# A decode kernel bound by its loads: fixed transpose buffers, a finer last block, and 256 rows of w_down loaded onto partitions 0 to 63 alone

## The chip, the cores and the metric

The kernel runs on one core of a Trainium2 chip. The metric is device time in microseconds (us) of one execution; every number of a run is a median with the lowest and highest execution beside it. One core draws its loads through sixteen DMA engines (the page of a profile counts 16). The trace does not name them; the numbers 0 to 15 in this text are names. The tensor engine is PE, the vector engine DVE, the scalar engine ACT, GpSimd POOL and the sync engine SP; SP issues nearly all loads here.

## The reference

For four tokens, `g * a + (1 - g) * b`. Cut to what matters:

```python
# A: attention over a cache: B=4, H=32 heads, 8192 cached positions, Dh=128, D=1024
q = (x @ wq)                                   # wq 1024 x 4096
p = softmax(q . k_cache / sqrt(128))           # k_cache, v_cache: 4 x 32 x 8192 x 128 bf16, 268 MB each
a = (p . v_cache) @ wo                         # wo 4096 x 1024
# B: one token per row, so every token is selected: F = 3584
b = x + sigmoid(x @ w_r) * ((silu(x @ w_gate) * (x @ w_up)) @ w_down)      # w_down 3584 x 1024
g = sigmoid((x * gate_w).sum(-1))
```

The inputs are 576 MB, nearly all of it the two caches, and each byte is used once.

## The kernel before

The program streams everything through a ring of five 4 MB buffers ("slots"). K loads and V loads alternate; the weights of part B are put in among the first of them ("side"), and `wo` comes last. Cut to what the change touches:

```python
ring = ctx.enter_context(tc.tile_pool(name="ring", bufs=5))      # 128 partitions x 32 KB each
ttp = ctx.enter_context(tc.tile_pool(name="ttp", bufs=2))        # transpose outputs, from a pool

def k_piece(u):
    ...
    kn = slot()
    nc.sync.dma_start(out=kn[:], in_=kv_view(A_k_cache, u))      # 4 MB: 128 rows of 32 KB
    for c in range(JR // CJ):                                    # 4 per piece, 256 in all
        T = ttp.tile([P, CJ, 2, 32, 2], BF, name="T", tag="T")
        nc.vector.transpose(out=T[:]..., in_=kn[:, c * CJ * Dh:(c + 1) * CJ * Dh]...)
        ...                                                      # matmuls on T

def wd_piece(g0, ng):                                            # w_down: ng groups of 512 rows
    w = slot()[:, :ng * FR * D]...
    nc.sync.dma_start(out=..., in_=wdv[:, g0:g0 + ng]...)        # 4 rows (8 KB) per partition and group
    ...                                                          # matmuls against hT

side = [..., lambda: (gu_piece(wuv, 1, TW), h_done()), lambda: wd_piece(0, 4), lambda: wd_piece(4, FG - 4)]
...
last = [wo_block(g) for g in range(2, NWB - 2)]                  # wo: 512 rows of 2 KB a block
last += [wo_block(g, r, r + FR // 2) for g in (NWB - 2, NWB - 1) for r in (0, FR // 2)]   # four halves
...
for use in last:
    use()                                                        # matmuls on wo, into acc
res = const.tile([Bn, D], BF)
nc.vector.tensor_copy(out=res[:, 0:NB], in_=acc[:, 0:NB])
nc.sync.dma_start(out=out2[:, 0:NB], in_=res[:, 0:NB])
... # the other half of res through ACT
```

## Time and profile before

| | before |
|---|---|
| time | 1349.41 us (1349.39 to 1349.46, 3 runs) |
| profiled execution | 1349.57 us, span 1347.8 us |
| DMA busy | 90% or more in 39 of 40 slices |
| PE, DVE busy | 79%, 47% |
| DMA rate | 428 GB/s, mean of the span |

These are lines of the profile's page of the kernel before. Part 2 cuts the span into 40 slices: one digit a slice is the busy share in tenths, and GB/s is what the sixteen engines moved. Part 3 has one line a DMA queue: packets, MB, share of the time of sixteen engines.

```profile
span 1347.8 us, 8253 instructions
...
PE   2667779876978868876998769888788859797878
...
DMA  9999999999999999999999999999999999999997
GB/s 403 433 433 422 433 430 430 432 433 430 430 433 430 430 431 434 429 431 432 433 428 432 433 430 430 433 431 429 432 434 429 428 433 434 429 428 434 432 423 323
DMA packets 22162, 576.22 MB, mean 428 GB/s; under 512 B 2399, under 2 KB 2407, under 8 KB 2925
...
q1 hardware_dynamic: 22104, 575.68, 99.5%
q8 instruction: 27, 0.44, 0.1%
q14 instruction: 11, 0.08, 0.0%
```

DMA is at 9 throughout and the rate is flat at about 431 GB/s: the loads bound the kernel, and compute hides under them. Only the last slice falls to 7 and 323 GB/s. Queue 1 carries the data; queues 8 and 14 carry the program itself, 27 and 11 packets of instructions. By its count queue 8 is taken to be the tensor engine's program (27 packets; the page has 4600 and 2412 instructions on PE and PEld); of queue 14, the five packets that fall together on one engine are taken to be DVE's.

The timeline of the kernel before, from 1342.3 us on, shows what comes after the last load (start, duration, engine, line, operation, in brackets the idle time before it and what ended it):

```profile
1342.57 1.02 PE L188 MATMUL acc<-piece,LT 128*4 128x512 bf16 x4 [0.17 <-DMA piece<-in_A_wo_dram]
...
1343.81 1.02 PE L188 MATMUL acc<-piece,LT 128*4 128x512 bf16 x4 [0.22 <-DMA piece<-in_A_wo_dram]
...
1344.66 0.68 DVE L461 CAST res<-acc 4x512 bf16<-4x512 f32 x1 [8.20 <-PE acc L188]
1344.87 0.57 ACT L463 CAST res<-acc 4x512 bf16<-4x512 f32 x1 [13.41 <-PE acc L188]
```

PE waits for the last half block of `wo`, which lands at 1343.77 us, then does four matmuls, and 4.1 us after the landing the span ends. So the span is "when the last load lands" plus 4.1 us.

**When does a load land?** Of each load onto all 128 partitions the trace has sixteen completion records, taken to be one from each engine. The distance from first to last record tells how far the engines have drifted apart. It was 1.2 us at the start of the stream, 2.1 at 258 us, 5.0 at 1133 us and 6.5 at the last transfer: the first engine is done at 1337.26 and the last at 1343.77. Six microseconds lie between the early engines and the late ones, and only the latest counts.

**Who is late?** Packet records of the trace carry a queue, a size, a start and a duration, but no engine. I reconstructed the engines by chaining packets, each starting where one of its engine ended. In the chains of before, three engines carry no instruction packets and end at 1336.8 to 1337.1 us; the eight that carry queue 8 in turn end at 1341.5 to 1341.8 (three packets) and 1342.9 to 1343.4 (four packets); one with five packets of queue 14 ends at 1342.8. So each queue-8 packet (16 KB; about 1.0 to 1.1 us itself) costs its engine about 1.5 us. From one 4 MB load to the next, the sixteen records keep their distances, except that one of them falls back by 1.52 to 1.56 us where a packet of queue 8 lies (20 of the 27 packets can be read so in the kernel before), and one by 0.95 to 0.98 us at each of the five packets that are taken to be DVE's. The record of a landing comes 0.4 to 0.5 us after its engine's last packet, so an end in the chains (1343.4) and a landing (1343.77) are not the same number.

That the packets of queue 8 go round eight engines can be seen without any chaining, from the durations of its 27 packets. Every eighth has nearly the same duration, but for the very first (ns, kernel before; the columns are turns 1 to 8):

```
turn       1     2     3     4     5     6     7     8
         964  1018  1026  1081  1069  1061  1100  1108
        1094  1018  1018  1073  1068  1061  1100  1099
        1095  1018  1018  1074  1069  1060  1099  1107
        1094  1018  1020
```

27 is three rounds and three more, so the engines of turns 1 to 3 have a fourth packet. Two neighbours in the ring are set apart by their 1013 to 1026 ns; they will be called the short pair.

### The profile page before, as it was taken

The page shows a single profiled execution, that of the slowest core. Times are in us where ns is not written, and L with a number is a line of the kernel's source. Part 1 is how long each engine was busy: PE and PEld are TensorE (multiplying, and loading weights), DVE is VectorE, ACT ScalarE, POOL GpSimd, SP SyncE. Part 2 cuts the span into 40 slices and gives each one's busy share as a digit, 9 for nine tenths or more (in the row PEclk, how much of TensorE's full clock was granted, in tenths as well). Part 3 has the DMA queues.
Part 4 walks back from the last instruction along what each step waited for, and adds up shares of the span by engine and source line. Part 5 has one row for each costly group of instructions (what it writes and reads, how often), then busy time and mean ns, then how long its engine had stood idle before and what let it go on. Part 6 is the DMA issues. An engine that isn't in the chain of part 4 may idle for free.

```text
span 1347.8 us, 8253 instructions
## 1 busy us (share of the span) xinstructions
PE 1059.3 (79%) x4600; PEld 233.2 (17%) x2412; DVE 631.4 (47%) x375; ACT 41.5 (3%) x46; POOL 47.9 (4%) x115
## 2 busy tenths in 40 slices
PE   2667779876978868876998769888788859797878
PEld 0111111211111111111212111211112112121111
DVE  3555755535544554454545454444544456346000
ACT  0000010001000010001000010000000010000000
POOL 2000000000000000000000000000000000000000
PEclk8878989898989989989898879899888979999899
DMA  9999999999999999999999999999999999999997
GB/s 403 433 433 422 433 430 430 432 433 430 430 433 430 430 431 434 429 431 432 433 428 432 433 430 430 433 431 429 432 434 429 428 433 434 429 428 434 432 423 323
DMA packets 22162, 576.22 MB, mean 428 GB/s; under 512 B 2399, under 2 KB 2407, under 8 KB 2925
## 3 DMA queue, kind: packets, MB, share of 16 engines
q1 hardware_dynamic: 22104, 575.68, 99.5%
q8 instruction: 27, 0.44, 0.1%
q14 instruction: 11, 0.08, 0.0%
q10 hardware_dynamic: 20, 0.02, 0.0%
HBM read 575.68 MB, written 0.01 MB: 427 GB/s over the span
## 4 chain that ended last, share of the span: by engine, by line
DMA 50%; PE 30%; DVE 11%; issue 6%; ACT 1%; POOL 1%; SPq 0%; DVEq 0%; ACTq 0%
DMA piece<-in_A_k_cache_dram 40%; PE o_ps L401 16%; PE S_ps L342 13%; DVE T L336 10%; DMA piece<-in_A_v_cache_dram 9%; PE small L419 1%; DMA piece<-in_A_wo_dram 1%; POOL PB L373 1%; DVE PT L367 1%; ACT PTs L365 1%; ACT OS L411 1%; DVE OS L412 1%; POOL tot L377 0%; PE acc L188 0%; PE o_ps L225 0%
## 5 line engine op out<-in xcount | busy, mean ns | idle before, releaser
L336 DVE STREAM_TRANSPOSE T<-piece 128x2048 uint32<-128x2048 uint32 x256 | 576.1, 2288 | 437.0 <-DMA piece<-in_A_k_cache_dram 321.1
L342 PE MATMUL S_ps<-T,Z 128*128 128x512 bf16 x2048 | 544.6, 416 | 246.6 <-DVE T L336 235.3
L401 PE MATMUL o_ps<-piece,PB 128*16 128x512 bf16 x2048 | 457.6, 382 | 14.8 <-DMA piece<-in_A_v_cache_dram 14.8
L342 PEld LDWEIGHTS <-Z 128*128 128x128 bf16 x1024 | 108.0, 105 | 667.2 <-issue 664.3
L401 PEld LDWEIGHTS <-PB 128*16 128x16 bf16 x1024 | 91.9, 90 | 373.1 <-issue 361.3
L412 DVE SCALAR_TENSOR_TENSOR OS<-o_ps,mE,OS 128x512 f32<-128x512 f32 x16 | 12.0, 751 | 174.6 <-ACT OS L411 174.6
L326 POOL TENSOR_TENSOR Z<-qa,mq 128x16 bf16<-128x16 bf16 x64 | 16.7, 262 | 1072.3 <-PE S_ps L342 1054.3
L411 ACT ACTIVATE OS<-o_ps,mE 128x512 f32<-128x512 f32 x16 | 11.0, 687 | 1040.5 <-PE o_ps L401 1040.5
L419 PEld LDWEIGHTS small<-selg,OS 128*128 128x128 f32 x128 | 24.9, 273 | 12.2 <-issue 11.1
L419 PE MATMUL small<-selg,OS 128*128 128x8 f32 x128 | 22.3, 302 | 0.0
L353 DVE TENSOR_REDUCE m<-S_ps 128x1 f32<-128x1024 f32 x8 | 9.8, 1225 | 15.9 <-PE S_ps L342 15.9
L188 PE MATMUL acc<-piece,LT 128*4 128x512 bf16 x64 | 14.9, 378 | 1.7 <-DMA piece<-in_A_wo_dram 1.6
L373 POOL COPY PB<-PT 64x1024 bf16<-64x1024 bf16 x8 | 15.1, 1884 | 29.1 <-DVE rex L375 29.1
L372 ACT COPY PB<-PT 64x1024 bf16<-64x1024 bf16 x8 | 15.3, 1908 | 10.6 <-DVE PT L367 10.6
L367 DVE STREAM_TRANSPOSE PT<-PTs 128x1024 bf16<-128x1024 bf16 x8 | 10.0, 1245 | 11.9 <-ACT PTs L365 11.9
L188 PE MATMUL acc<-piece,hT 128*4 128x512 bf16 x56 | 12.4, 379 | 0.0
L131 PE MATMUL small<-identb,x 6*128 6x6 bf16 x8 | 0.6, 194 | 14.2 <-DVE identb L128 14.2
L379 DVE RECIPROCAL rinv<-tot 128x16 f32<-128x16 f32 x8 | 2.0, 253 | 19.9 <-POOL tot L377 19.9
L365 ACT ACTIVATE PTs<-S_ps,negm 128x1024 bf16<-128x1024 f32 x8 | 8.9, 1113 | 70.0 <-DVE negm L362 70.0
L225 PE MATMUL S_ps<-piece,xw 128*4 128x512 bf16 x64 | 6.6, 591 | 3.0 <-DMA piece<-in_A_wq_dram 3.0
L422 DVE SCALAR_TENSOR_TENSOR OT<-small,sgb,rinv 128x8 bf16<-128x8 f32 x16 | 3.2, 202 | 11.7 <-PE small L419 11.7
L358 POOL PARTITION_ALL_REDUCE gmx<-mex x8 | 3.1, 390 | 81.9 <-issue 50.3
(72 smaller groups left out, 74.6 us busy)
## 6 DMA issues: line engine op xcount, KB each, us to landing
piece<-in_A_k_cache_dram SPq DMA_DIRECT2D x64, 4096.0 KB, 39.4
piece<-in_A_v_cache_dram SPq DMA_DIRECT2D x63, 4096.0 KB, 39.1
piece<-in_A_wq_dram SPq DMA_DIRECT2D x2, 4096.0 KB, 22.1
piece<-in_B_w_gate_dram SPq DMA_DIRECT2D x2, 3584.0 KB, 40.1
piece<-in_B_w_up_dram SPq DMA_DIRECT2D x2, 3584.0 KB, 34.6
piece<-in_A_wo_dram SPq DMA_DIRECT2D x6, 1024.0 KB
piece<-in_B_w_down_dram SPq DMA_DIRECT2D x1, 4096.0 KB, 35.6
piece<-in_A_v_cache_dram SPq DMA_DIRECT2D x4, 1024.0 KB, 32.6
```

The costliest lines, as they stand in the source:

```text
L188: nc.tensor.matmul(out_ap, lhsT=lhsT, rhs=rhs, start=start, stop=True, skip_group_check=True)
L326: nc.gpsimd.tensor_tensor(out=Z[:, :, 31:31 + P].rearrange("p e (s d c) -> p e s d c", s=HT, d=QH)[:, :, :, :, 0], in0=qa[:, :, h0:h0 + HT ...
L336: nc.vector.transpose(out=T[:].rearrange("p j h i e -> p (j h i e)").bitcast(U32), in_=kn[:, c * CJ * Dh:(c + 1) * CJ * Dh].bitcast(U32))
L342: nc.tensor.matmul(sps[:, z, :], lhsT=Z[:, he, s:s + P], rhs=T[:, 16 * z:16 * z + 16, half, :, e], start=(t == 0 and c == 0 and he == 0), ...
L365: nc.scalar.activation(out=PTs[:], in_=sps[:].rearrange("p z n -> p (z n)"), func=ACT.Exp, bias=negm[:, 0:1], scale=scale, accum_out=rs[:, ...
L367: nc.vector.transpose(out=PT[:].rearrange("p j i -> p (j i)"), in_=PTs[:])
L372: nc.scalar.copy(out=Bv[0:W, :, :, 0, :], in_=Pv[0:W])
L373: nc.gpsimd.tensor_copy(out=Bv[W:P, :, :, 1, :], in_=Pv[W:P])
L401: nc.tensor.matmul(o_ps[row:row + NM, e, :], lhsT=B_[:, JT * t + c, z, w].rearrange("p e s j -> p (e s j)"), rhs=vn[:, j0 * Dh:(j0 + 4) * ...
L411: nc.scalar.activation(out=o_sb[:], in_=o_ps[:, 0, :], func=ACT.Copy, scale=mE[:, 0:1])
L412: nc.vector.scalar_tensor_tensor(out=o_sb[:], in0=o_ps[:, 1, :], scalar=mE[:, 1:2], in1=o_sb[:], op0=ALU.mult, op1=ALU.add)
L419: nc.tensor.matmul(oT[:, :], lhsT=o_sb[:, q * Dh:(q + 1) * Dh], rhs=selg[:, q].rearrange("p t s -> p (t s)"), start=(q == 0), stop=(q == 3))
```

## The change

The intent has three parts. (1) The transposes write two fixed buffers rather than tiles of a pool, with the write-after-write order of a buffer's two users left to the waits that its readers need anyhow; this saves semaphore instructions on DVE (236 to 61 in the built program). (2) The last 512 rows of `w_down` are no longer 4 rows on each of 128 partitions: 256 rows stay on all partitions (2 rows each), and 256 rows go to partitions 0 to 63 (4 rows, 8 KB each), in two times four transfers of eight partitions. The author took these transfers to fall on the same eight engines each time, so that the other eight carry less. (3) The last half block of `wo` is loaded as two quarters, so that two matmuls rather than four follow the last landing.

```diff
-    ttp = ctx.enter_context(tc.tile_pool(name="ttp", bufs=2))
+    Tt = [const.tile([P, CJ * P], BF, name=f"T{i}") for i in range(2)]
+    turned = []
+    def turn(in_ap):
+        T = Tt[len(turned) % 2]
+        i = nc.vector.transpose(out=T[:].bitcast(U32), in_=in_ap.bitcast(U32)).ins
+        if len(turned) >= 2:
+            tc.declare_no_dep(i, turned[-2], reason="its readers are waited for")
+        turned.append(i)
+        return T[:].rearrange("p (j h i e) -> p j h i e", j=CJ, h=2, i=32)
 ... (other users of the pool's tiles take parts of Tt)
+    hTh = const.tile([P, 2, Bn], BF)
+    hTe = const.tile([P // 2, FR, Bn], BF)
 ... (h_done also transposes h for these two)
+    def wd_rest(g0):
+        w = slot()
 ...
+        nc.sync.dma_start(out=wa..., in_=wdv[:, g0:FG - 1]...)            # two whole groups
+        nc.sync.dma_start(out=wb..., in_=B_w_down[f0:f0 + 256]...)        # 2 rows a partition
+        def eighths(p0):
+            src = B_w_down[f0 + 256:f0 + 512].rearrange("(p r) n -> p (r n)", r=FR)
+            for i in range(4):
+                sl = slice(p0 + i, p0 + 32, 4)
+                nc.sync.dma_start(out=wc[sl].rearrange("p r n -> p (r n)"), in_=src[sl])
 ...
+        eighths(0)
+        side.insert(0, lambda: (eighths(32), use()))
 ...
-            lambda: (gu_piece(wuv, 1, TW), h_done()), lambda: wd_piece(0, 4), lambda: wd_piece(4, FG - 4)]
+            lambda: (gu_piece(wuv, 1, TW), h_done()), lambda: wd_piece(0, 4), lambda: wd_rest(4)]
 ...
-    last += [wo_block(g, r, r + FR // 2) for g in (NWB - 2, NWB - 1) for r in (0, FR // 2)]
+    last += [wo_block(NWB - 2, 0, 2), wo_block(NWB - 2, 2, 4)]
+    last += [wo_block(NWB - 1, 0, 2), wo_block(NWB - 1, 2, 3), wo_block(NWB - 1, 3, 4)]
```

More of the change, by code (lines that the diff above doesn't have):

```diff
@@ L194, in gates @@
         rg_ps = small([P, 2, Bn])
-        wrep = ttp.tile([P, 2, DT, P], BF, name="wrep", tag="T")
+        wrep = Tt[0][:, 0:2 * DT * P].rearrange("p (w t d) -> p w t d", w=2, t=DT)
         for i in range(2):
@@ L205, in add_x @@
     def add_x():
-        xf = ttp.tile([Bn, D], F32, name="xf", tag="T")
-        nc.vector.tensor_copy(out=xf[:], in_=x6[0:Bn])
+        xf = Tt[len(turned) % 2][0:Bn, 0:2 * D].bitcast(F32)
+        nc.vector.tensor_copy(out=xf, in_=x6[0:Bn])
         for n in range(NH):
@@ L233, in q_done @@
     def q_done():
-        qs = ttp.tile([P, 2, 4, P], BF, name="qs", tag="T")
-        nc.vector.tensor_copy(out=qs[:].rearrange("p z c d -> p z (c d)"), in_=q_ps[:])
+        qs = Tt[1][:, 0:1024].rearrange("p (z c d) -> p z c d", z=2, c=4)
+        nc.vector.tensor_copy(out=qs.rearrange("p z c d -> p z (c d)"), in_=q_ps[:])
         qt = small([P, 2, 4, 4, 32], BF)
@@ L253, in h_done @@
     def h_done():
-        h = ttp.tile([P, 2, 512], F32, name="h", tag="T")
-        nc.scalar.activation(out=h[:], in_=o_ps[:], func=ACT.Silu)
-        nc.vector.tensor_tensor(out=h[:], in0=h[:], in1=acc4[:], op=ALU.mult)
+        h = Tt[len(turned) % 2][:, 0:2048].bitcast(F32).rearrange("p (z n) -> p z n", z=2)
+        nc.scalar.activation(out=h, in_=o_ps[:], func=ACT.Silu)
+        nc.vector.tensor_tensor(out=h, in0=h, in1=acc4[:], op=ALU.mult)
         for z in range(2):
@@ L260, in h_done @@
                 nc.tensor.transpose(out=ht[:, r].rearrange("p k i -> p (k i)"), in_=h[:, z, r:512:FR], identity=ident[:])
-            kn = min(4, FG - 4 * z)
+            kn = min(4, FG - 1 - 4 * z)
             for r in range(FR):
@@ L264, in h_done, with use @@
                                         in1=c12[:, 1:2, :].to_broadcast([P, kn, Bn]), op=ALU.mult)
+        k6 = (FG - 1) % 4
+        for dst, rows, c0, nr in ((hTh, P, 0, 2), (hTe, P // 2, 256, FR)):
+            ht = small([rows, nr, 4, 32])
+            for r in range(nr):
+                nc.tensor.transpose(out=ht[:, r].rearrange("p k i -> p (k i)"), in_=h[:, 1, c0 + r:c0 + 256:nr],
+                                    identity=ident[:])
+            nc.vector.tensor_tensor(out=dst[:], in0=ht[:, :, k6, 0:Bn],
+                                    in1=c12[0:rows, 1:2, :].to_broadcast([rows, nr, Bn]), op=ALU.mult)
+    def wd_rest(g0):
+        w = slot()
+        f0 = P * FR * (FG - 1)
+        n2 = FG - 1 - g0
+        wa = w[:, 0:n2 * FR * D].rearrange("p (g r n) -> p g r n", g=n2, r=FR)
+        wb = w[:, n2 * FR * D:(n2 * FR + 2) * D].rearrange("p (r n) -> p r n", r=2)
+        wc = w[0:P // 2, (n2 * FR + 2) * D:(n2 * FR + 6) * D].rearrange("p (r n) -> p r n", r=FR)
+        nc.sync.dma_start(out=wa.rearrange("p g r n -> p g (r n)"),
+                          in_=wdv[:, g0:FG - 1].rearrange("f g r n -> f g (r n)"))
+        nc.sync.dma_start(out=wb.rearrange("p r n -> p (r n)"),
+                          in_=B_w_down[f0:f0 + 256].rearrange("(p r) n -> p (r n)", r=2))
+        def eighths(p0):
[3 more added lines that the diff above has]
+                nc.sync.dma_start(out=wc[sl].rearrange("p r n -> p (r n)"), in_=src[sl])
+        def use():
+            for lhs, rhs in [(hT[:, g0 + g, r, :], wa[:, g, r]) for g in range(n2) for r in range(FR)] \
+                    + [(hTh[:, r, :], wb[:, r]) for r in range(2)] + [(hTe[:, r, :], wc[:, r]) for r in range(FR)]:
+                for n in range(NH):
+                    mm_acc(acc[:, n * NB:(n + 1) * NB], lhs, rhs[:, n * NB:(n + 1) * NB])
+        eighths(0)
+        side.insert(0, lambda: (eighths(32), use()))
     def wd_piece(g0, ng):
@@ L334, in k_piece @@
         for c in range(JR // CJ):
-            T = ttp.tile([P, CJ, 2, 32, 2], BF, name="T", tag="T")
-            nc.vector.transpose(out=T[:].rearrange("p j h i e -> p (j h i e)").bitcast(U32),
-                                in_=kn[:, c * CJ * Dh:(c + 1) * CJ * Dh].bitcast(U32))
+            T = turn(kn[:, c * CJ * Dh:(c + 1) * CJ * Dh])
             s = 31 - (JT * t + c)
```

## The prediction

> **What bounds the kernel.** The DMA engines. The page's slices show them 90% or more busy in 39 of 40, 428 GB/s on average; the tensor engine 79%. A 32 KB packet takes 1.215 us (median of the packet records), and no engine's chain of packets shows a gap, so faster compute in the middle buys nothing. Each big DMA ends with 16 completion records, one per engine. First to last they lie 1.2 us apart at 12 us, 3.4 at 433, 5.0 at 1133 and 6.5 for the last transfer (seven engines by 1339.3 us, nine at 1342.0 to 1343.8). After the slowest come 1.0 us of four matmuls (timeline: 1343.81), a copy, the output, end at 1347.8.
>
> **Why engines lag.** The spread jumps at instruction fetches. Queue 8 fetches 27 times 16 KB[...]. Chaining packets end to start (my reconstruction; the trace names no engine), these rotate over eight engines, three or four each, about 1.6 us lost per fetch. A ninth engine carries five 8 KB fetches of queue 14[...], 1.2 us each: it ends at 1342.8, the slowest at 1343.4.[...]
>
> **What the change does.**
> 1. Fixed transpose buffers: the built program drops 175 vector-engine semaphore instructions (236 to 61); the engine's total goes from 616 to 443, so five fetches become three. That takes about 2.4 us off the ninth engine.
> 2. 256 rows of w_down (512 KB) move from all partitions to 0 to 63. [...] So engines 0 to 7 carry eight more 8 KB packets minus the halved rest: +1.2 us; engines 8 to 15 carry 1.2 us less (8 x 312 ns become 8 x 159 ns). If 8 to 15 are the fetching eight, their ends fall from 1341.5-1343.4 to 1340.3-1342.2; the ninth goes to about 1341.6, the early ones to at most 1340.3.
> 3. Finer end: the last half-block becomes two quarters: two matmuls after the last landing, not four, -0.4 us; eight more packets of 2 KB cost +0.1 us.
> 4. Costs: ten more transfers, some transposes, a slot held longer; the small transfers' semaphores delay one K load to when w_down's rest has landed, leaving about 10 us of queued work instead of 39. I expect no gap.
>
> **Sum:** -1.2 + 0.1 - 0.4, about -1.5 us: **1347.9 us**, range 1346.9 to 1349.3. Chances: faster by over 2% 0.005, within 2% 0.99, slower 0.005.
>
> **What would show it right.** Queue 8 stays near 27 fetches; queue 14 loses two; total bytes unchanged; the last transfers' completion spread falls from 6.5 to about 4 us or less; DMA stays 9s around 60 to 130 us; after the last landing two matmuls.
>
> **What would make it wrong.** The fetching engines are not 8 to 15: then slow engines gain load, +1 us. The delayed K load starves the queue near 100 us: some us slower. The ninth engine turns out slowest after +1.2 us: gain about 0.5.

The sum came to -1.2 + 0.1 - 0.4 = -1.5 us, from 1349.4 to 1347.9. But the -1.2 rests on an assumption, that transfers of eight rows all fall on one and the same eight engines and leave out the other eight; its "0 to 7" and "8 to 15" can be read as names for these two halves. The times in it are the trace's (medians on queue 1: 312 ns for a packet of 8 KB, 160 ns for one of 4 KB). What the trace of before shows of small transfers are counts: the load of x, of four rows, has four packets of 2 KB and four completion packets of 4 bytes. That 443 instructions of DVE make three fetches was an estimate too (616 had made five). For the +0.1 the profile after has 84 ns for a packet of 2 KB and 159 for one of 4 KB, so sixteen for eight come to 0.07 us an engine.

## The result, and the profile after

Ratios in this text are the mean time of one kernel's fast runs over that of the other's fast runs of the same rounds, so they are not quite the ratio of the medians quoted.

| | before | after |
|---|---|---|
| time, median (lowest to highest) | 1349.40 (1349.26 to 1349.46), 6 runs | 1349.35 (1348.65 to 1350.13), 6 runs |
| ratio | | 1.000, 95% interval 0.9987 to 1.0013 |

The time is the same. But the six executions after are not scattered around 1349.35: they are 1348.65, 1348.72, 1348.74 and 1349.95, 1350.03, 1350.13. There are **two levels**, 1.3 us apart, one below the kernel before and one above it, and the median falls between. The profiled execution was one of the lower level.

The page of the profile after, the same lines:

```profile
span 1347.0 us, 8114 instructions
...
PE   3667669876978868886998769788688869887788
...
DMA  9999999999999999999999999999999999999998
GB/s 401 433 430 427 430 428 435 432 429 431 433 432 429 433 432 429 432 433 430 430 433 433 428 432 433 433 429 431 430 433 433 431 427 433 436 431 425 434 425 334
DMA packets 22447, 576.21 MB, mean 428 GB/s; under 512 B 2494, under 2 KB 2502, under 8 KB 3276
...
q1 hardware_dynamic: 22392, 575.68, 99.6%
q8 instruction: 27, 0.44, 0.1%
q14 instruction: 8, 0.07, 0.0%
```

Queue 8 kept its 27 packets. Queue 14 lost two packets of 8 KB, as predicted: those taken to be DVE's are three rather than five. (The page counts 8 packets rather than 11; the third is one of 96 bytes that lies 0.13 us after the start of the span before and 0.07 us ahead of it after.) The completion packets of 4 bytes on queue 1 show the small transfers: 2388 before, which is sixteen for each of 149 loads onto all partitions and four for an output of four rows; 2484 after, 96 more, which is sixteen for each of two further such loads and eight for each of the eight transfers of eight rows. The bytes are the same, and DMA stays at 9 where the small transfers are (about 130 to 155 us, the fourth and fifth slice: 427 and 430 GB/s). The end, from the timeline after, from 1342.3 us on:

```profile
1342.07 1.89 PE L202 MATMUL acc<-piece,LT 128*4 128x512 bf16 x8
...
1343.78 0.68 DVE L511 CAST res<-acc 4x512 bf16<-4x512 f32 x1 [7.78 <-PE acc L202]
1343.99 0.57 ACT L513 CAST res<-acc 4x512 bf16<-4x512 f32 x1 [12.99 <-PE acc L202]
```

The last load lands at 1343.31 and the copies start 0.47 us later rather than 0.89; the span ends 3.7 us after the landing rather than 4.1. The finer end works as meant.

What did not work is the landing. The completion records of the last transfer, in order (us after 1330):

```
before         7.3  7.3  7.6  8.5 ... twelve more, up to 13.77    first to last 6.51
after, lower   6.3  6.6  9.0  9.7 ... twelve more, up to 13.31    first to last 7.02
```

The drift was to shrink from 6.5 to about 4 us. It grew. The two earliest records became earlier still, by 1.0 and 0.7 us, where nothing was to be gained, and the latest came down by 0.46 us only. In the reconstructed chains of this execution the two latest engines, at 1342.7 and 1342.8, are two that carry three packets of queue 8 *and* eight of the moved packets. The six other engines of queue 8 carry none of them and end at 1340.3 to 1340.6 (three packets) or 1342.0 to 1342.1 (four), about 1.2 us earlier than in the kernel before, as predicted. So a theory suggested itself before any experiment: two of the eight fetching engines are among those that carry the moved rows.

That would also explain two levels (theory L). If the ring of queue 8 starts at another engine in another execution, the loaded two get sometimes three packets and sometimes four, and only loaded engines make the difference visible. Rivals: the fixed buffers or the finer end bring the two levels; or the small transfers slow the queue.

### The profile page after: what moved, and what is told of

It reads as the page before. It is cut to its first block, busy times and chain, and to the rows that moved or that the text cites. A ratio compares the mean times of both kernels' runs of the same rounds, so it can differ in the third digit from the quotient of the medians.

```text
span 1347.0 us, 8114 instructions
## 1 busy us (share of the span) xinstructions
PE 1064.0 (79%) x4610; PEld 234.2 (17%) x2420; DVE 632.3 (47%) x377; ACT 41.5 (3%) x46; POOL 48.0 (4%) x115
## 2 busy tenths in 40 slices
DMA packets 22447, 576.21 MB, mean 428 GB/s; under 512 B 2494, under 2 KB 2502, under 8 KB 3276
## 4 chain that ended last, share of the span: by engine, by line
DMA 47%; PE 33%; DVE 16%; ACT 1%; issue 1%; POOL 1%; SPq 0%; DVEq 0%; ACTq 0%
DMA piece<-in_A_k_cache_dram 36%; PE o_ps L450 16%; PE S_ps L391 15%; DVE T L117 14%; DMA piece<-in_A_v_cache_dram 5%; DMA piece<-in_B_w_down_dram 3%; DMA piece<-in_A_wq_dram 2%; DMA piece<-in_A_wo_dram 1%; PE small L468 1%; POOL PB L422 1%; PE acc L202 1%; DVE OS L461 1%; ACT PTs L414 1%; ACT OS L460 1%; DVE PT L416 1%
```

## The experiments

Twelve runs were made, two of them repeats of a kernel (3 and 11; number 6 stands for two runs). All computed correct results, also the marker kernel. Each call ran its kernels on one chip, beside runs of the kernel before on that chip: medians 1349.40, 1349.42, 1349.41 and 1349.47 us, all within 1349.20 to 1349.69.

### 1. Number the engines with marker loads

The trace names no engine, but engines can be told apart by what is put on them. In the profiles so far a transfer of one, four or eight rows has one, four or eight completion packets, and a load onto all 128 partitions sixteen. The author's assumption was that loads of 1 to 15 rows, of 256 bytes each, take 1 to 15 engines, and each load those of the shorter ones and one more. Then every engine gets a number of marker packets of its own, from 15 down to 0, that can be read off its chain. This text calls the engine with 15-m markers engine m. These numbers are names, and say nothing of how the chip numbers its engines.

```diff
+    mk = [const.tile([n, P], BF, name=f"mark{n}") for n in range(1, 16)]
+    def mark(n):
+        nc.sync.dma_start(out=mk[n - 1][:], in_=A_wo[0:n, 0:P])
 ...
             k_piece(u)
+            if 12 <= u < 27:
+                mark(u - 11)
```

> The kernel before plus fifteen marker loads in the middle of the stream, the n-th of n rows of 256 bytes[...]. Theory L (the end is set by the engines that also fetch instructions, and they are not all in 8 to 15): of the eight engines that take turns at queue 8, two have numbers under 8 and six have numbers of 8 or more, probably 6 to 13; the vector engine's fetches (queue 14) sit on one engine under 8. Rival F (the fetching eight are 8 to 15, as predicted, and something else ate the gain): all eight have seven or fewer markers. Time within 2 us of before under both.

Measured: 1349.57 us (one run), within the 1349.28 to 1349.65 of the nine runs of the kernel before beside it, so the markers disturb nothing that can be measured. The chains, by number of markers:

```
engine   queue-8 packets at (us; duration about)    queue-14 packets    end of data (us)
 14      39, 433, 838, 1236                                             1343.4
  5      86, 497, 885, 1279      (1018 to 1026 ns)                      1343.4
  6      137, ...                (1018 ns)                              (chain mixed up later)
  9      193, 586, 983                                                  1341.7
 10      236, 644, 1037                                                 1341.9
 11      290, 687, 1088                                                 1341.9
 12      342, 736, ...                                                  (later part mixed up)
 13      391, 798, 1182                                                 1341.8
  3                                                 five                1342.8
  0, 1, 4                                           0, 1, 2             1338.5 to 1338.7
  7, 8, 15                                          none                1337.0, 1337.2, 1337.4
```

The chain of engine 2 was lost near 445 us, and after that two chains are mixed in part; the numbers come from the stretch before it. The fetching engines are **5, 6, 9, 10, 11, 12, 13 and 14**, in a ring in the order 9, 10, 11, 12, 13, 14, 5, 6. Two of them, the short pair, are below 8. The expectation had the count right (two below 8) and guessed other numbers. The trace agrees with the assumption as far as it can: a load of n rows has n marker packets, and the chains fit engines that are nested, each load on those of the load before it and one more; they fit no other arrangement that I tried. Which engines carry the packets of queues 8 and 14 is thus read from these chains alone.

### 2. Everything but the move

```diff
-            lambda: (gu_piece(wuv, 1, TW), h_done()), lambda: wd_piece(0, 4), lambda: wd_rest(4)]
+            lambda: (gu_piece(wuv, 1, TW), h_done()), lambda: wd_piece(0, 4), lambda: wd_piece(4, FG - 4)]
 (and h_done as before)
```

> The changed kernel without the move of w_down: fixed buffers and finer end alone. Theory L: the slowest engine is still one with four fetches of queue 8, so the last landing stays within 0.2 us of before; the finer end saves about 0.35 us after it: 1349.0 to 1349.2 us, on one level (all runs within 0.3 us), because three of the eight engines have four fetches whichever the turn starts with. Rival B (the two levels of the changed kernel, 1348.7 and 1350.0, come from the fixed buffers or the finer end): two levels about 1.3 us apart here too.

Measured: 1349.46 us (1349.30 to 1349.57, 5 runs), ratio 1.000, interval 0.9988 to 1.0013. **One level.** So the two levels come with the move. The time missed the expectation by 0.3 us: the span fell to 1347.3 to 1347.5, as it should with the finer end, but the time of an execution lies 2.05 us above its span instead of 1.7. What those 0.3 us outside the span are, the profile does not show (see 6). The last landing is 1343.82, as in the kernel before (1343.77), although the engine with DVE's instructions now ends at about 1340.4: four-packet engines of queue 8 stand in for it, at 1343.1 to 1343.4.

### 3. The changed kernel again, hoping for a profile of the upper level

> The changed kernel once more. Theory L: two levels, about 1348.7 and 1350.0 us. On the upper one an engine that got more of w_down also has four fetches of queue 8, on the lower one it has three; the profile's time must agree with its count. With three neighbours of eight having the fourth fetch and two of the eight on the loaded side, about half of the runs are on the upper level. Rival B or a stall at the small transfers: the level has nothing to do with the turn of the fetches.

Measured: 1349.94, 1348.66, 1348.61, 1349.99, 1348.56 us: the same two levels. The profile fell on 1349.94, the upper one. The durations of queue 8's 27 packets, in ns, in turns 1 to 8, of the two profiled executions of one and the same program:

```
turn              1     2     3     4     5     6     7     8
lower level     961  1107  1086  1018  1026  1082  1078  1060
               1108  1099  1082  1016  1026  1073  1069  1061
               1108  1099  1093  1018  1013  1201  1073  1060
               1099  1099  1087
upper level     947  1015  1018  1073  1076  1068  1099  1099
               1094  1018  1018  1074  1068  1058  1100  1100
               1094  1020  1026  1073  1069  1066  1096  1107
               1087  1016  1025
```

(One packet of the lower level, 1201 ns at turn 6, is out of line.) In the lower level the short pair, engines 5 and 6, is at turns 4 and 5 and has three packets each. In the upper level it is at turns 2 and 3 and has four. The ring is the same, its start is not. In the chains the pair ends at 1344.0 us in the upper level, where it ended at 1342.7 and 1342.8 in the lower. The timeline of the upper level's profile, from 1343 us on:

```profile
1342.77 2.39 PE L202 MATMUL acc<-piece,LT 128*4 128x512 bf16 x9
...
1344.98 0.68 DVE L511 CAST res<-acc 4x512 bf16<-4x512 f32 x1 [7.75 <-PE acc L202]
1345.19 0.57 ACT L513 CAST res<-acc 4x512 bf16<-4x512 f32 x1 [12.93 <-PE acc L202]
```

The first copy starts at 1344.98 rather than 1343.78: all of the 1.2 us between the levels is the last landing (1344.51 against 1343.31). (A packet of queue 8 costs its engine 1.5 us in a single step, so 0.3 us of the fourth packet do not show in this difference; why is not known.) Theory L is borne out in two profiles; its confirmation by taking the load off the pair is run 10.

### 4. Engines 0 to 5, with six rows a transfer

This kernel was drawn up together with run 1, before the numbers were known. If the ring was 6 to 13, as guessed then, the moved rows should go to engines 0 to 5 only: ten transfers of six partitions at a stride of ten, and one of four.

```diff
-            for i in range(4):
-                sl = slice(p0 + i, p0 + 32, 4)
+            for sl in parts:
                 nc.sync.dma_start(out=wc[sl].rearrange("p r n -> p (r n)"), in_=src[sl])
+        six = [slice(i, 60, 10) for i in range(10)] + [slice(60, 64)]
-        eighths(0)
-        side.insert(0, lambda: (eighths(32), use()))
+        sixths(six[:5])
+        side.insert(0, lambda: (sixths(six[5:]), use()))
```

> The changed kernel with the 256 rows sent by ten transfers of six partitions and one of four, instead of eight of eight: same bytes, same partitions[...]. Theory L with the fetching engines at 6 to 13: every fetching engine loses 1.2 us, none gains; engines 0 to 5 gain about 2.0 us and end at 1342.5 us at the latest (the one with the vector engine's fetches): one level at 1347.9 to 1348.4 us. If partitions rather than engine numbers count, or if the small transfers stall the stream: no better than the changed kernel, 1348.7 to 1350.0 on two levels.

Measured: 1353.43 us (1353.03 to 1354.51, 5 runs), ratio 1.0031: 4 us slower, a clear miss. This had nothing to do with instruction fetches. The fourth and fifth slice of its page (GB/s) show where:

```profile
GB/s 404 433 432 405 401 427 434 429 431 435 432 425 433 431 434 430 431 430 434 431 433 428 431 432 432 432 432 429 432 432 432 428 431 431 434 432 429 431 425 329
```

405 and 401 where the changed kernel has 427 and 430. Packets of the large loads were slow around the small transfers: 32 KB packets took up to 3.2 us instead of 1.215, and 84 of them over 1.24 us (11 in the changed kernel; table in 9). (Engine 5 is one of the ring by run 1, and one of the six that a load of six rows marks, so it would still carry moved rows; by the estimates, 2.0 us here and 1.2 in the changed kernel, that is 0.8 us more, the smaller part of this loss.)

### 5. The move alone

The kernel before plus the move; tiles from the pool and the coarse end as before.

> The kernel before with the move of w_down alone: pooled transpose buffers and the old end. Theory L: the engine of the vector engine's fetches (number 3 by the markers, below 8) still has five of them and now gets 1.2 us more, so it ends at about 1344.0 us in every run, as late as engines 5 and 6 do on the upper level. The two levels fall together: all runs at 1349.8 to 1350.4 us, 0.4 to 1.0 above before. If the fixed buffers do not matter to the end: two levels, about 1349.0 and 1350.3.

Measured: 1349.99 us (1349.56 to 1350.47, 5 runs), ratio 1.0004, interval 0.9992 to 1.0017. So the move alone does not help and, in its upper runs (1350.47 twice), costs 1 us. The expectation, all runs between 1349.8 and 1350.4, was met in part only: two runs lie below it (1349.56 and 1349.71) and two just above, so the levels came closer but did not fall together. The profile, with the short pair at turns 7 and 8, shows a last landing of 1344.13; in the chains the latest engine is the one with five packets of DVE's instructions, at 1343.7: it carries moved rows as well. That shows what the fixed buffers can do in this change, in the one execution profiled: they clear engine 3, but only with the move does engine 3 become the latest.

### 6. The finer end alone, and the fixed buffers alone

The edits are those parts of the diff above.

> The kernel before with the finer end alone. Span 0.3 us shorter in any case. If the 0.3 us that the run without the move lost outside the span come with the finer end: 1349.4, as before. If they do not: 1349.0 to 1349.15 us.

> The kernel before with the fixed buffers alone. Theory L: the vector engine's fetches fall from five to three, but the engine that carries them was not the slowest, so the last landing does not move: span as before within 0.15 us. If the 0.3 us outside the span come with the fixed buffers: 1349.7 us; if not: 1349.4.

Measured: finer end 1349.20 us (1349.10 to 1349.27, 5 runs), 0.2 us under the kernel before (1349.42, 9 runs, of which seven lie above all five of these); the span of the profiled run is 1347.5. Fixed buffers 1349.77 us (1349.75 to 1349.80, 5 runs), 0.35 us *above*. The span of the fixed buffers' run is 1347.7, no longer than that of before, and the time lies 2.05 us above it; so the 0.3 us outside the span come with the fixed buffers in runs 2 and 6. The changed kernel, which has them too, lies 1.71 us above its span in both profiled runs. I have no explanation for this, and it stays open. (The kernel of runs 10 and 11 lies 1.93 and 1.95 us above its span; its two profiles alone show an instruction packet of 8 KB after the end of the span, by 1.8 us. Runs 2 and 6 show none, so this does not explain theirs.) The last landing with the fixed buffers alone is 1343.67 us, with the engine of DVE's instructions two packets lighter in the chains (1340.4, from 1342.8): the gain that the prediction gave to the "ninth engine" is there and buys nothing by itself, because engines of queue 8 are later.

### 7. Engines 0 to 4, spread out in time

A second attempt at fewer engines, with one small transfer (five, three or two rows) after each of fifteen K loads rather than several in a row, into a buffer of its own. If the slowness of run 4 came from small transfers in a row or from the wait for a slot, it should go.

```diff
+    few = [slice(i, 50, 10) for i in range(10)] + [slice(50 + i, 62, 4) for i in range(4)] + [slice(62, 64)]
+    def wd_few(i):
 ...
+        nc.sync.dma_start(out=wc[few[i]].rearrange("p r n -> p (r n)"), in_=src[few[i]])
 ...
+            if 10 <= u < 10 + len(few):
+                wd_few(u - 10)
```

> The changed kernel with the 256 rows sent by ten transfers of five partitions, four of three and one of two, one at a time after each K load from the eleventh on, into a buffer of their own, so that none holds a slot or has to wait for the one ahead. By the markers engines 0 to 4 have no fetches of queue 8; they alone carry the rows now (3.1 us for engines 3 and 4, up to 4.6 us for 0 and 1, less 1.2). Theory L: all eight fetching engines lose 1.2 us whichever turn the fetches take, no engine ends after 1342.4 us: one level, 1347.9 to 1348.4 us, and no gap in the stream at 100 to 170 us. If the loss of the version with six-partition transfers came from small transfers as such and not from the queue running dry: again 1351 or more.

Measured: 1353.18 us (1352.67 to 1353.30, 5 runs), ratio 1.0027. Missed again by 5 us, and again by slow packets, now in small groups at each transfer: 599 packets of 32 KB over 1.24 us between 125 and 500 us, where the changed kernel has 11. So neither the row of small transfers nor the shared slot was it. What runs 4 and 7 have in common, and the changed kernel has not: the stride of ten, that is, the partitions on which the rows of one transfer lie. The next two runs change these partitions and keep the packets.

### 8. One edit: eight neighbouring partitions

The changed kernel's rows lie at a stride of four partitions, from partitions 0 to 3 and 32 to 35 on. The test gives each transfer eight neighbouring partitions, with the source rows that belong there, and changes nothing else: the number of packets (22447 on both pages, 2494 of them under 512 B), their sizes and their places in the queue are the same.

```diff
-                sl = slice(p0 + i, p0 + 32, 4)
+                sl = slice(p0 + 8 * i, p0 + 8 * i + 8)
```

> The changed kernel with one edit: each of its eight small transfers takes eight neighbouring partitions instead of every fourth. The same number of transfers, the same 8 KB packets, the same eight engines (each transfer has eight rows)[...]. Two kernels before this one (six and five partitions at a stride of ten) were 4 us slower because packets on all engines lengthened around the small transfers. [...]this one shows it too: 32 KB packets over 1.24 us near 130 to 160 us, 1 to 4 us slower than the changed kernel. If it does not (then the stride of the source, the number of rows or the moment do), it stays like the changed kernel: each execution at about 1348.7 or about 1350.0, span 1347.0 or 1348.2.

(The first outcome stands for "the partitions matter", the second for "they do not".)

Measured: 1354.69 us (1353.66 to 1355.94, 5 runs), ratio 1.0038, interval 1.0024 to 1.0051. One changed slice costs 5 us. So it matters which eight rows, and with them which partitions, go into one transfer; by what means is not shown. The GB/s line of its page:

```profile
GB/s 405 430 432 393 409 431 427 432 431 432 433 433 430 426 433 429 434 433 431 432 431 431 431 432 432 432 430 429 432 433 429 432 431 432 434 430 432 427 427 310
```

The fourth and fifth slice are at 393 and 409. 79 packets of 32 KB between 125 and 170 us are over 1.24 us, where the changed kernel has 2.

### 9. The changed kernel's stride, four partitions up

Run 8 changed both the spacing of a transfer's rows and the partitions on which they lie. To part these, the rows kept the stride of four and were moved up by four partitions (4 to 67, in a fixed buffer). The source rows and the packets are those of the changed kernel; run 10 has a fixed buffer as well and is not slow.

```diff
+    wc = const.tile([68, FR, D], BF)
+    nc.gpsimd.memset(wc[:], 0.0)
 ...
-                nc.sync.dma_start(out=wc[sl].rearrange("p r n -> p (r n)"), in_=src[sl])
+                nc.sync.dma_start(out=wc[p0 + i + 4:p0 + i + 33:4].rearrange("p r n -> p (r n)"), in_=src[sl])
 (hTe has 68 rows, of which the first four meet zeros; two constants live in Tt to make room)
```

> The changed kernel with its eight small transfers moved up by four partitions (partitions 4 to 67, in a fixed buffer)[...]. [...] this is as slow: about 1354, 60 to 80 packets of 32 KB over 1.24 us near 130 to 160 us. [...]it is like the changed kernel, 1348.7 or 1350.0, with 1 or 2 such packets.

(The first outcome, as slow as run 8, is for the place of the rows as the cause, the second for their spacing.)

Measured: 1354.45, 1354.63, 1351.10, 1351.19 us (ratio 1.0021, interval 1.0006 to 1.0036). Two levels once more, both above those of the changed kernel, by 2.4 and 4.5 us. Its line, the profile being of the upper level:

```profile
GB/s 403 432 432 408 414 430 432 430 432 430 432 432 433 432 430 431 429 433 433 429 433 431 432 432 430 432 431 431 432 431 432 429 431 432 433 433 430 429 426 296
```

So the stride of four is not enough: the same rows four partitions up slow packets too. How much, all in one table: over all packets of queue 1 that start between 120 and 500 us, the time above the median of their size in the whole run, summed and divided by sixteen engines. (A median that is 1 ns higher takes 0.3 us off a figure, so 0.6 and 0.9 are the same.)

| kernel | us per engine | packets of 32 KB over 1.24 us |
|---|---|---|
| before | 0.9 | 11 |
| changed kernel, lower and upper level | 0.9, 0.9 | 11, 11 |
| 128 rows in transfers of four, stride of four from 0 to 3 and 32 to 35 on (run 10) | 0.6 | 10 |
| six rows at a stride of ten (run 4) | 4.9 | 84 |
| five rows at a stride of ten (run 7) | 4.2 | 599 |
| eight neighbours (run 8) | 5.4 | 88 |
| stride of four, moved up by four (run 9) | 3.5 | 89 |

Run 8's figure is 1.9 us above run 9's, so close spacing may add something; a run that parts the two in the other way was not made. For run 9 the table accounts for 2.5 us of the 4.5 in the upper level: its first engine is done 2.8 us later than the changed kernel's, the latest 4.5 us later, and why the late ones lose more I have not found out.

### 10 and 11. The dose halved, onto engines 0 to 3

With the ring known, the move can be aimed. 128 rows move rather than 256, in eight transfers of four rows, so that engines 0 to 3, those that a load of four rows marks, carry them, none of which is in the ring; the rows lie on partitions 0 to 15 and 32 to 47, at the stride of four that cost nothing in the changed kernel. The other 384 rows of the group lie 3 on a partition.

```diff
-    hTh = const.tile([P, 2, Bn], BF)
-    hTe = const.tile([P // 2, FR, Bn], BF)
+    hTh = const.tile([P, 3, Bn], BF)
+    hTe = const.tile([48, FR, Bn], BF)
+    wc = const.tile([48, FR, D], BF)          # both zeroed; partitions 16 to 31 stay zero
 ...
-                          in_=B_w_down[f0:f0 + 256].rearrange("(p r) n -> p (r n)", r=2))
+                          in_=B_w_down[f0:f0 + 384].rearrange("(p r) n -> p (r n)", r=3))
         def eighths(p0):
-            src = B_w_down[f0 + 256:f0 + 512].rearrange("(p r) n -> p (r n)", r=FR)
-            for i in range(4):
-                sl = slice(p0 + i, p0 + 32, 4)
-                nc.sync.dma_start(out=wc[sl].rearrange("p r n -> p (r n)"), in_=src[sl])
+            r0 = f0 + 384 + 2 * p0
+            src = B_w_down[r0:r0 + 64].rearrange("(p r) n -> p (r n)", r=FR)
+            for i in range(4):
+                nc.sync.dma_start(out=wc[p0 + i:p0 + 16:4].rearrange("p r n -> p (r n)"), in_=src[i:16:4])
```

> The changed kernel with the dose halved and the target narrowed: 128 rows instead of 256 move, in eight transfers of four partitions (8 KB packets), so that only engines 0 to 3 carry them, which by the markers' run carry none of the tensor engine's fetches[...]. The buffer of the rows is a fixed one, so two constants moved into the transpose buffers. Engines 0 to 3 gain eight packets of 0.31 us and lose 8 times 0.08 us: +1.9 us; all others, the eight fetching ones among them, lose 0.6 us. Theory of the fetching engines 5, 6, 9 to 14: last landing 0.6 us earlier than in the kernel with fixed buffers and finer end alone (1343.8), about 1343.2 in every execution, engine 3 with the vector engine's three fetches at about 1342.3; times of one level, 1348.5 to 1348.9, and no upper level at 1350.0. Rival (the two levels come from the transposed buffers or the chip, not from where the bytes go): two levels about 1.3 us apart again. If 4-row transfers slow packets as five- and six-row ones did, 2 us slower.

Measured: 1348.67 us (1348.43 to 1349.19, 5 runs), ratio 0.9995, interval 0.9983 to 1.0008. The profiled run's span is 1346.6 us, its last landing 1342.89. There is no run near 1350.0. There were two sublevels, 1348.43 to 1348.67 and 1349.09 to 1349.19, so the kernel was run again:

> The kernel with 128 rows on engines 0 to 3 once more, for the interval and for its two sublevels of 1348.5 and 1349.1 (the profile of the first run fell on the lower). Expected: again five times between 1348.4 and 1349.2, none at 1350.0; last landing near 1342.9 in the lower, 0.5 us later in the upper sublevel if the profile falls there.

Measured: 1348.73 us (1348.52 to 1348.85, 5 runs), ratio 0.9995, interval 0.9982 to 1.0007, last landing 1343.17; one level this time. The upper sublevel of the first five has no profile and stays unexplained. The lines of the page of run 10 that answer to those above:

```profile
span 1346.6 us, 8130 instructions
...
GB/s 402 436 430 426 429 434 431 429 432 433 430 432 432 431 431 430 432 433 430 432 430 434 432 429 432 433 429 431 433 432 427 434 433 429 429 435 433 429 425 335
```

426 and 429 in the fourth and fifth slice: no slow stretch. Its page has 2462 packets under 512 B, 32 fewer than that of the changed kernel: four completion packets a small transfer instead of eight. All ten runs (1348.43 to 1349.19) are below all eighteen runs of the kernel before beside them (1349.29 to 1349.64). The gain of 0.7 us is 0.05%, and the interval of the ratio, which allows for more than the scatter, does not exclude 1. By its median it is the fastest kernel (the lower level of the changed kernel is as fast); no bigger gain should be claimed for it.

## Why the prediction was wrong

The prediction was 1347.9 us, range 1346.9 to 1349.3; the median was 1349.35. Two levels, 1348.7 and 1350.0, lie around it; the lower is inside the range. Point by point:

- **"The DMA engines bound it; the end is set by the engines that lag, and they lag by instruction fetches"**: right. The 1.2 us between two executions of one program go with one packet of 16 KB more on each of two engines (run 3).
- **"The ninth engine: five fetches become three, -2.4 us"**: right. Queue 14 lost two packets of 8 KB, and in the chains that engine ended at 1340.4 rather than 1342.8 with the fixed buffers alone (run 6). By the steps of the completion records, 0.95 to 0.98 us each, the two packets account for 1.9 of these 2.4 us; the rest is not explained. It is worth nothing there, and counts only where the move loads that engine (run 5).
- **"Engines 0 to 7 carry +1.2 us, engines 8 to 15 carry 1.2 us less"**: right. The ring's six engines above 7 end at 1340.3 to 1342.1 rather than 1341.5 to 1343.4, and engines 5 and 6 have eight of the moved packets each in the chains.
- **"If 8 to 15 are the fetching eight, their ends fall from 1341.5-1343.4 to 1340.3-1342.2"**: **this step failed.** It carried the whole term of -1.2 us. The fetching eight are 5, 6 and 9 to 14 (run 1). Engines 5 and 6 gained 1.2 us on top of their fetches and became the latest. The last landing moved not by -1.1 us (-1.2 for the engines, +0.1 for the smaller packets) but by -0.46 us when these two have three fetches, and by +0.74 when they have four. The prediction named this as what would make it wrong, "+1 us", but took the even split as its central case with nothing in the trace to say which engines were which. It could have been known to be open: the chains gave a count, not numbers. And it assumed one fixed ring; that its start differs between executions of one program was in no term.
- **"Finer end: -0.4, +0.1"**: right within 0.2. Landing to end of span 4.1 us became 3.7 us in both levels; alone, it gained 0.2 us, and its last landing (1343.78) shows nothing of the 0.1 us for smaller packets (run 6).
- **"I expect no gap"**: right. One K load waited 9.3 us in its queue for `w_down` and was issued at 116.88 us, yet the K loads around the small transfers land at their usual distance of 9.7 us (first records at 130.95, 140.72, 150.43 us).
- **"The spread falls from 6.5 to about 4"**: wrong, in consequence: 7.0 and 8.3.

The sum for the lower level closes: landing -0.46, after the landing -0.35 gives -0.8 us, and the profiled executions differ by 0.83 (1349.57 and 1348.74). For the upper level +0.74 and -0.35 give +0.4; measured 1349.94 against 1349.57.

Shown by runs: which engines fetch (chains, numbered by markers), that the levels need the move (runs 2, 6) and follow the place of engines 5 and 6 in the ring (run 3), that with the load on engines 0 to 3 the upper level goes and the landing falls by 0.6 to 0.9 us (runs 10, 11), that small transfers of the same packets slow the stream or do not by the partitions on which their rows lie (runs 8, 9: 88 and 89 packets of 32 KB over 1.24 us, against 11; in the upper level of run 9 the first engine is done 2.8 us later and the latest 4.5). Not shown: why some partitions cost this and others do not, and which engine writes which partitions. Open: the 0.3 us outside the span with fixed buffers; the sublevels of run 10; why the ring starts where it does (in fourteen profiles the short pair was at turns 2 and 3 six times, 7 and 8 six times, 4 and 5 twice, and nowhere else).

## What to carry to other kernels

When sixteen engines share a stream, the slowest decides (here the last of sixteen records lay 6.5 us after the first, and the span ended 4.1 us after it); before moving bytes off "the slow ones", number them, for example with loads of 1 to 15 rows, which cost nothing measurable here (1349.57 us). When a kernel's repeats fall into two groups, look at each group by itself: here the median said "no change" while the program gained 0.7 us in one and lost 0.6 in the other. And when a transfer has few rows, try where they lie: with eight rows at a stride of four, from partitions 0 to 3 and 32 to 35 on, the stream had no more slow packets than before, while the same rows on eight neighbouring partitions cost 5 us and four partitions further up 2.4 to 4.5.
